# Joining the key-value sums of batches 2 and 3 with neighbouring matmul groups, and loading their q and k into the narrowing's memory

## The chip, the cores and the metric

The kernel runs on one core of one Trainium2 chip. The metric is the time of one execution on the device in microseconds (us), the median of several runs. The engines are named as in the profile: PE is TensorE, DVE is VectorE, ACT is ScalarE, POOL is GpSimd, and SP is SyncE, which here issues DMAs only.

## What is computed

The reference has two parts, one after the other. The first is an attention with polynomial sketches over 4 batches and 4 heads, with 1088 positions of 32 values:

```python
def phi(x):
    a = np.einsum('rd,bhsd->bhsr', S1, x)      # r = 8
    b = np.einsum('rd,bhsd->bhsr', S2, x)
    return np.einsum('bhsi,bhsj->bhsij', a, b).reshape(*x.shape[:-1], r * r)
q_p, k_p = (phi(q), phi(k))
kv = np.einsum('bhsf,bhsd->bhfd', k_p, v)
z = np.sum(k_p, axis=2)
num = np.einsum('bhsf,bhfd->bhsd', q_p, kv)
den = np.einsum('bhsf,bhf->bhs', q_p, z)[..., None] + 1e-06
attn = num / den
```

The second takes the result as 4352 tokens of 128 values (`x`) through a gated layer with 1536 inner columns:

```python
gate = 1.0 / (1.0 + np.exp(-(x @ w_gate)))
val = x @ w_val
out = gate * val @ w_out
```

All of it is in 32-bit floats. The inputs arrive as 64-bit numbers, so the weights are narrowed on the chip first.

## The kernel before

**The gated layer sets the rhythm.** The tokens are cut into chunks of 512 (the last has 256). For each chunk, the 1536 inner columns are taken in blocks of 128. One block of one chunk is a wave: `w1` multiplies `xT` with the blocks of `w_gate` and `w_val` into a PSUM tile `wave` (line 540), ACT takes the sigmoid (line 548), and DVE multiplies the two into `g` (`glu`, line 583). There are 12 waves in a chunk and 102 in all. Counting starts at 0, so chunk 2 is waves 24 to 35. The PSUM pool `psm` has two buffers for `wave` tiles, and two small groups of attention matmuls (`cqps` and `nps`) take a turn in it as well.

**The second product follows later.** For chunks 1 to 7, `w2_a` and `w2_b` multiply `g` with `w_out` in seven half-sized products in place of eight (`prod`, line 377). They need sums of token halves, which POOL makes (`tsum`, line 367). They run three and four waves after the second wave of a pair. When a chunk is complete, DVE puts the pieces together in several small sums and two transposes (lines 479 and 514, tiles `res` and `o_sb`). These stand in the list `moe["late"]`, and one entry is taken per wave.

**The order is written by hand.** The program fixes the order of PE, DVE, ACT and POOL. The order in which SP issues its DMAs is chosen by a planner. `slot(group, waves)` first emits a group of attention work, then for each wave the `glu` of the wave before, one entry of `late`, the second products that are due, and the next wave. `until(n)` emits waves until n have been emitted, so a step after `until(n)` stands on DVE between `glu(n-2)` and `glu(n-1)`. Here "slot n" is the place just ahead of wave n. A chunk's waves may start only when its tokens are in `xT`.

**Attention of one batch** passes through these steps:

- `load_kq` and `load_v` fetch k, q and v. The tile for k and q (tag `kq`, one buffer) is also the tile `bq` of the q features.
- `turn_k` and `turn_q` transpose k and q on DVE (lines 642 and 653).
- `begin`: `kps` projects k in 16 matmul records (line 673), and DVE transposes the result into `kab`. `qcomp` projects q (`cqps`, line 819), ACT copies the result to `cq`, and `spread` writes it to DRAM (`dq`) and reads it back repeated, in 14 DMAs on SP, into `qp`, `bq`, `a8` and `b8`.
- `outer` makes the k features on DVE (line 752, twice). `sum_z` adds them up over positions (line 926, one instruction and then three).
- `kv` multiplies the features with v (lines 892 and 901) into a tile of the PSUM pool `ps2` (tag `two`, one buffer of two banks). `kvd` copies that out on ACT (line 914).
- `ndt` transposes the copy (lines 957 and 965). `weights_z` prepares the denominators' weights on DVE (lines 1001 to 1008).
- `qmult` completes the q features on DVE (line 872, twice).
- `parts` makes the denominators (`den_j`, line 1021, with a DVE product at line 1029, then line 1034), the numerators (line 1258), and the quotients in `xT`.

**The plan of batches 2 and 3** is a table of wave numbers, one for each of `turn_k`, `turn_q` twice, `begin`, `outer` twice, `sum_z` twice, `kv`, `qmult` with `ndt` and `weights_z`, `qmult`, and `parts`:

```python
plan = {2: (27, 29, 30, 31, 32, 34, 36, 37, 38, 39, 42, 44)}
plan[3] = (48, 49, 51, 53, 56, 57, 58, 59, 60, 61, 63, 68)
```

**The narrowing** of the weights works in the tiles `cap`, `tail` and `head` of the pool `sbN`, until a step in the waves of chunk 0 completes the last block. The pool stays reserved to the end.

**At the start** `warm` issues matmuls with constants, whose result nobody reads.

Of the kernel before, what the change touches and what calls it, by code (L numbers as in the profile page):

```python
# [16 lines left out]
P = 128  # L17
# [3 lines left out]
def kernel(  # L21
# [31 lines left out]
    ld = ctx.enter_context(tc.tile_pool(name="ld", bufs=1))  # L53
    sbA = ctx.enter_context(tc.tile_pool(name="sbA", bufs=2))
    raw = ctx.enter_context(tc.tile_pool(name="raw", bufs=NJ // 2))
    sbN = ctx.enter_context(tc.tile_pool(name="sbN", bufs=1))
    sbG = ctx.enter_context(tc.tile_pool(name="sbG", bufs=3))

    dram = ctx.enter_context(tc.tile_pool(name="dram", bufs=1, space=bass.MemoryType.DRAM))

# [203 lines left out]
    k_t, q_t = {}, {}  # L264


    def new_kq(b):
        t = ld.tile([P, 2 * H * W1], F32, tag="kq", name="kq")
        kq = t[:, : 2 * T * D].rearrange("p (a t d) -> p a t d", a=2, t=T)
        k_t[b], q_t[b] = kq[:, 0], kq[:, 1]  # L270

# [20 lines left out]
    def warm(*cols):  # L292
        t = psm.tile([P, 2, 512], F32, tag="wave", name="warm")
        x = nc.const_aps.tensor(1.0, [P, P], F32)
        for n in cols:
            r = nc.const_aps.tensor(1.0, [P, n], F32)
            nc.tensor.matmul(out=t[:, 0, :n], lhsT=x, rhs=r, start=True, stop=True)  # L297
# [312 lines left out]
    def slot(group, waves, behind=None):  # L610

        if group is not None:
            group()
        todo = moe["todo"]
        for _ in range(waves):
            more = moe["ci"] < len(tok_chk)
            if more and sum(tok_chk[moe["ci"]]) > moe["ready"]:
                break
            glu()
            for _ in range(2 if moe["ci"] >= len(tok_chk) - 1 else 1):  # L620
                if moe["late"]:
                    moe["late"].pop(0)()
            while todo and todo[0][0] <= moe["n"]:
                todo.pop(0)[1]()
            if behind is not None:
                behind()
                behind = None
            if more:
                w1()
            elif not todo:  # L630
                break
            else:
                todo.pop(0)[1]()
# [26 lines left out]
    WD = 160  # L660
    mask = {}

    def kps(b):
        t = ps2.tile([P, 2, 512], F32, tag="two", name="kps")
        ts = [t[:, 0], t[:, 1]]
        turns = [(g, pi) for g in range(4) for pi in range(2)]

        if b == 0:
            ts[1] = pso.tile([P, TCH], F32, tag="acc1", name="kps1")
            turns.sort(key=lambda x: x[1])  # L670
        for g, pi in turns:
            rows = slice(64 * pi, 64 * pi + 64)
            nc.tensor.matmul(  # L673
                out=ts[pi][32 * g : 32 * g + 32, : NJK * 32],
                lhsT=sk[rows, :],
                rhs=kT_of[b][rows, KBASE[g] : KBASE[g] + NJK],
                start=True,
                stop=True,
            )

        KAB[b] = sbA.tile([P, 2, NJK, 32], F32, tag="kab", name="kab")
        for pi in range(2):
            nc.vector.transpose(
                out=KAB[b][:, pi].rearrange("p j c -> p (j c)"), in_=ts[pi][:, : NJK * 32]
            )
        KP[b] = sbA.tile([P, 2, NJK, 2, F], F32, tag="kp", name="kp", bufs=1)
# [147 lines left out]
    def spread(b, ns, cq, put, get):  # L834
        p0 = 64 * ns[0]
        d = dram.tile([P, 2, W1], F32, tag="dq", name="dq")
        put.dma_start(out=d[p0:], in_=cq[p0:])
        for n in ns:
            for i, t in enumerate((QP[b], BQ[b])):

                for c in (0, 1) if i else (0,):
                    d0 = d[64 * n + 32 * c + 2 * i, 0]
                    rows = [[0, R], [8 * W1, R]] if i else [[8 * W1, 2 * R], [0, R]]
                    get.dma_start(  # L844
                        out=t[64 * c : 64 * c + 64 if i else P, n * H * W1 : (n + 1) * H * W1],
                        in_=bass.AP(
                            tensor=d0.tensor, offset=d0.offset, ap=rows + [[1, H * W1]]
                        ),
                    )
        if len(ns) < 2:  # L850
            return
        put = get

        B8[b] = sbA.tile([P, W1], F32, tag="b8", name="b8", bufs=1)
        A8[b] = sbA.tile([P, 2, WD], F32, tag="a8", name="a8", bufs=1)
        for x in range(2):
            for m in range(2):
                p0 = 64 * x + 32 * m
                for i, t in enumerate((A8[b], B8[b])):
                    d0 = d[2 * i + m, 0]  # L860
                    if i == 0:
                        offset, run = d0.offset + (W1 - WD) * x, [[W1, 2], [1, WD]]
                    else:
                        offset, run = d0.offset + W1 * x, [[1, W1]]
                    put.dma_start(
                        out=t[p0 : p0 + 32],
                        in_=bass.AP(tensor=d0.tensor, offset=offset, ap=[[8 * W1, 32]] + run),
                    )
# [16 lines left out]
                    skip_group_check=True,  # L885
                )

    def kv(b, zsum):
        kvz = KVZ[b] = ps2.tile([P, 2, 512], F32, tag="two", name="kvz")[:, 0]
        for j in [1, 2, 3, 4, 5, 6, 7, 8, 0]:  # L890
            for h in range(H):
                nc.tensor.matmul(  # L892
                    out=kvz[32 * h : 32 * h + 32, :F],
                    lhsT=v_sb[:, h, j, :],
                    rhs=KP[b][:, h // 2, j, h % 2, :],
                    start=(j == 1),
                    stop=(j == 0),
                    skip_group_check=True,
                )
        for h in range(H):  # L900
            nc.tensor.matmul(
                out=kvz[32 * h : 32 * h + 32, F : 2 * F],
                lhsT=nc.const_aps.tensor(1.0, [P, 32], F32),
                rhs=zsum[:, h, :],
                start=False,
                stop=True,
                skip_group_check=True,
            )
# [104 lines left out]
        )  # L1013


    def den_j(b):
        t = ps2.tile([P, 2, 512], F32, tag="two", name="denj")
        for pi in range(2):
            rows = slice(64 * pi, 64 * pi + 64)
            for x in range(4):  # L1020
                nc.tensor.matmul(  # L1021
                    out=t[32 * x : 32 * x + 32, pi, :WD],
                    lhsT=ZW[b][rows, 4 * (x % 2) : 4 * (x % 2) + 4].rearrange("p x i -> p (x i)"),
                    rhs=B8[b][rows, (W1 - WD) * (x // 2) : (W1 - WD) * (x // 2) + WD],
                    start=True,
                    stop=True,
                )
        PD[b] = sbA.tile([P, 2, WD], F32, tag="pd", name="pd", bufs=1)
        nc.vector.tensor_tensor(out=PD[b], in0=t[:, :, :WD], in1=A8[b], op=MUL)


    def den_i(b, dps):
# [118 lines left out]
        start=True,  # L1151
        stop=True,
    )
    warm(64)
    st_ = st_[:, : 2 * R].rearrange("p (n r) -> p n r", n=2)
    sk = const.tile([P, 2, 2, R], F32, tag="sk")
    nc.vector.tensor_tensor(
# [71 lines left out]
    slot(None, 1)  # L1229
    cq = {}  # L1230

    def begin(b):
        glu()
        kps(b)
        cq[b] = qcomp(b, (0, 1), (psm, "wave"))
        spread(b, (0, 1), cq[b], nc.scalar, nc.sync)

# [6 lines left out]
    def part01(first):  # L1244
        glu()
        late.append(dn(0, 1)(first=first, later=True))
# [16 lines left out]
                    stop=True,  # L1263
                )

    def parts(b):
        den_j(b)
        glu()
        t = psm.tile([P, 2, 512], F32, tag="wave", name="nps")
        numerators(b, t, False)  # L1270
# [38 lines left out]
    load_kq(1)  # L1309
    slot(None, 1)  # L1310
    slot(lambda: part01(lambda: narrow_w(NJ - 1, 3)), 1)
    slot(last01, 1)
    load_v(1)
    turn_k(1)
    slot(None, 1)
    turn_q(1, 0)
# [14 lines left out]
    slot(lambda: ndt(1), 1)  # L1331
    slot(None, 1)
    qmult(1, 1)
    load_kq(2)
    slot(None, 1)
    slot(lambda: parts(1), 1)
    moe["store"]()
# [1 line left out]
    def until(n):  # L1339
        slot(None, n - moe["n"])  # L1340

    plan = {2: (27, 29, 30, 31, 32, 34, 36, 37, 38, 39, 42, 44)}
    plan[3] = (48, 49, 51, 53, 56, 57, 58, 59, 60, 61, 63, 68)
    for b in range(2, B):
        at = iter(plan[b])
        until(next(at))
        turn_k(b)
        for n in range(2):
            until(next(at))
            turn_q(b, n)  # L1350
        until(next(at))
        slot(lambda: begin(b), 1)
        for pi in range(2):
            until(next(at))
            outer(b, pi)
        for step in range(2):
            until(next(at))
            sum_z(b, step)
        until(next(at))
        slot(lambda: kv_all(b), 1)  # L1360
        if b + 1 < B:
            load_v(b + 1)
        until(next(at))
        qmult(b, 0)
        slot(lambda: ndt(b), 1)
        weights_z(b)
        until(next(at))
        qmult(b, 1)
        load_kq(b + 1)
        until(next(at))  # L1370
        slot(lambda: parts(b), 1)
    slot(None, 10**3)


# [28 lines left out]
```

## Time and profile before

| | |
|---|---|
| median of 3 runs | 292.19 us (292.1 to 292.46) |
| profiled execution, its own time | 296.02 us |
| span of the profiled execution, first to last instruction | 294.1 us |
| PE busy | 288.8 us, 98% of the span |
| DVE busy | 186.5 us, 63% |
| POOL busy | 160.6 us, 55% |
| ACT busy | 93.7 us, 32% |
| DMA | 24.23 MB, mean 82 GB/s |
| granted clock of PE, mean | 0.999 |

The busy times come from one profiled execution. Its own time is longer than the median of the runs, so its durations are read against its own span. Matmuls overlap, and the ends of their rows are modelled. For PE, therefore, the distances between starts say more than the sums of durations. A row of the order in time has the start from the span's beginning, the duration, the engine, the line, the operation, what it writes and reads, and in brackets how long the engine was idle before it and what ended that.

### The profile page before, as it was taken

The numbers are of one execution on the slowest core, as the hardware profiler recorded it, in microseconds if no ns is written. First come the engines' busy times: TensorE is split into PE (matmuls) and PEld (weight loads), VectorE is DVE, ScalarE is ACT, GpSimd is POOL, SyncE is SP. The second block draws the span as 40 slices with busy tenths as digits, with TensorE's granted clock in tenths as the row PEclk, the third lists the DMA queues.
The fourth block names the chain that finished last, engine by engine and source line by source line (L and its number), as shares of the span: only waits on it lengthen the run. The fifth ranks groups of instructions, "written<-read, shape, count | busy, mean of one in ns | idle before, by whom it ended". The sixth has DMA issues, their size and how long they took to land.

```text
span 294.1 us, 5762 instructions
## 1 busy us (share of the span) xinstructions
PE 288.8 (98%) x2264; PEld 156.6 (53%) x2264; DVE 186.5 (63%) x316; ACT 93.7 (32%) x172; POOL 160.6 (55%) x222
## 2 busy tenths in 40 slices
PE   8989999999999999999999999999999999999995
PEld 3543433355455455545555555554555555555895
DVE  5778789885656766677556696667436423552482
ACT  3386542321324222323224222323223223322321
POOL 2266544796535657655456498555456565646300
PEclk9999999999999999999999999999999999999999
DMA  7993613295640168416000474202000200020003
GB/s 219 347 336 68 150 39 125 74 180 137 186 97 0 19 163 159 133 50 177 12 0 2 129 174 106 37 0 38 1 0 2 36 2 0 0 31 7 0 4 54
DMA packets 28890, 24.23 MB, mean 82 GB/s; under 512 B 18560, under 2 KB 24064, under 8 KB 28864
## 3 DMA queue, kind: packets, MB, share of 16 engines
q1 hardware_dynamic: 25808, 21.95, 30.1%
q10 hardware_dynamic: 3056, 1.92, 2.3%
q8 instruction: 18, 0.29, 0.4%
q14 instruction: 8, 0.07, 0.1%
HBM read 20.60 MB, written 3.26 MB: 81 GB/s over the span
## 4 chain that ended last, share of the span: by engine, by line
PE 89%; DMA 7%; SPq 1%; DVE 0%; issue 0%; ACT 0%; DVEq 0%
PE wave L540 55%; PE prod L377 20%; DMA bq<-dq 5%; PE moeout L421 4%; PE moeout L447 2%; PE warm L297 1%; PE kps L673 1%; SPq L844 1%; PE nps L1258 1%; DMA s_in<-in_S_dram 1%; PE kvz L892 1%; PE cqps L819 1%; DMA dq<-cq 1%; DMA b<-dq 1%; PE denj L1021 0%; PE dps L1063 0%
## 5 line engine op out<-in xcount | busy, mean ns | idle before, releaser
L540 PE MATMUL wave<-xT,w_sb 128*64 128x512 f32 (+3 forms) x820 | 210.6, 566 | 0.0
L540 PEld LDWEIGHTS wave<-xT,w_sb 128*64 128x64 f32 (+1 forms) x820 | 85.4, 140 | 63.2 <-issue 51.0
L548 ACT ACTIVATE sg<-wave 128x512 f32<-128x512 f32 x102 | 60.9, 597 | 171.1 <-PE wave L540 163.2
L583 DVE TENSOR_TENSOR g<-wave,sg 128x512 f32<-128x512 f32 x96 | 65.9, 686 | 76.3 <-ACT sg L548 75.0
L367 POOL TENSOR_TENSOR tsum<-g 128x256 f32<-128x256 f32 x84 | 67.9, 810 | 29.7 <-DVE g L583 29.6
L367 POOL TENSOR_TENSOR tsum<-g,tsum 128x256 f32<-128x256 f32 x42 | 34.2, 814 | 57.8 <-DVE g L583 57.6
L377 PE MATMUL prod<-tsum,ws 128*64 128x256 f32 x252 | 62.8, 381 | 0.0
L377 PEld LDWEIGHTS prod<-tsum,ws 128*64 128x64 f32 x252 | 31.2, 137 | 16.0 <-issue 11.8
L377 PE MATMUL prod<-g,w_sb 128*64 128x256 f32 x168 | 34.7, 381 | 0.0
L367 POOL TENSOR_TENSOR tsum<-tsum,g 128x256 f32<-128x256 f32 x42 | 32.7, 779 | 3.3
L377 PE MATMUL prod<-tsum,w_sb 128*64 128x256 f32 x84 | 25.3, 383 | 0.0
L377 PEld LDWEIGHTS prod<-g,w_sb 128*64 128x64 f32 x168 | 16.0, 136 | 17.5 <-issue 14.7
L377 PE MATMUL prod<-g,ws 128*64 128x256 f32 x84 | 25.0, 379 | 0.0
L117 POOL TENSOR_TENSOR head<-head,tail 128x384 int32<-128x384 int32 (+1 forms) x10 | 9.9, 987 | 13.9 <-DVE head L111 12.6
L377 PEld LDWEIGHTS prod<-g,ws 128*64 128x64 f32 x84 | 11.5, 137 | 3.7
L421 PE MATMUL moeout<-g,w_sb 128*128 128x512 f32 (+1 forms) x28 | 12.5, 603 | 0.0
L377 PEld LDWEIGHTS prod<-tsum,w_sb 128*64 128x64 f32 x84 | 10.8, 137 | 3.0 <-issue 2.2
L872 DVE TENSOR_TENSOR qp<-qp,bq 128x1152 f32<-128x1152 f32 (+1 forms) x7 | 9.4, 1344 | 4.6 <-DMA a<-dq 4.6
L752 DVE TENSOR_TENSOR kp<-kab 128x1152 f32<-128x1152 f32 (+2 forms) x10 | 10.9, 1101 | 0.0
L576 DVE TENSOR_TENSOR g<-wave,sg 128x512 f32<-128x512 f32 x6 | 6.7, 1121 | 4.6 <-ACT sg L548 4.6
L479 DVE TENSOR_TENSOR res<-prod,other 64x512 f32<-64x512 f32 (+1 forms) x14 | 7.6, 544 | 3.1 <-DMA a<-dq 1.6
L514 DVE STREAM_TRANSPOSE o_sb<-res 64x512 f32<-64x512 f32 x14 | 9.6, 688 | 0.0
(129 smaller groups left out, 209.6 us busy)
## 6 DMA issues: line engine op xcount, KB each, us to landing
qp<-dq SPq DMA_DIRECT2D x7, 576.0 KB
bq<-dq SPq DMA_DIRECT2D x14, 288.0 KB
kq<-in_k_dram SPq DMA_DIRECT2D x3, 544.0 KB
kq<-in_q_dram SPq DMA_DIRECT2D x3, 544.0 KB
w_in<-in_moe_w_out_dram SPq DMA_DIRECT2D x6, 256.0 KB
w_in<-in_moe_w_gate_dram SPq DMA_DIRECT2D x5, 256.0 KB
w_in<-in_moe_w_val_dram SPq DMA_DIRECT2D x5, 256.0 KB
v<-in_v_dram SPq DMA_DIRECT2D x8, 144.0 KB
```

The source lines that it names most:

```text
L117: nc.gpsimd.tensor_tensor(out=head, in0=head, in1=tail, op=ALU.add)
L367: nc.gpsimd.tensor_tensor(out=t[:, u], in0=in0, in1=in1, op=ALU.subtract)
L377: nc.tensor.matmul(out=out, lhsT=lhsT, rhs=rhs, start=start, stop=stop, skip_group_check=True)
L421: nc.tensor.matmul(out=moe["acc"][d], lhsT=w_sb[:, 2, j, d], rhs=g[:, jj], start=(j == 0), stop=(j == NJ - 1),)
L479: nc.vector.tensor_tensor(out=out, in0=in0, in1=in1, op=op)
L514: nc.vector.transpose(out=o_sb[:64, d].rearrange("p t x -> p (t x)"), in_=r[:, 1 + 2 * d : 3 + 2 * d].rearrange("p u x -> p (u x)"),)
L540: nc.tensor.matmul(out=wv[d, which, jj * tw + o : jj * tw + o + tp], lhsT=w_sb[:, which, j0 + jj, d], rhs=xT[:, t0 + o : t0 + o + tp], sta ...
L548: nc.scalar.activation(out=sg, in_=wv[:, 0], func=ACTF.Sigmoid)
L576: nc.vector.tensor_tensor(out=g.rearrange("p (j u s y) -> p j y u s", j=2, u=2, y=4), in0=wv[:, 1].rearrange("p (j y u s) -> p j y u s", j ...
L583: nc.vector.tensor_tensor(out=g, in0=wv[:, 1], in1=sg, op=MUL)
L752: eng.tensor_tensor(out=KP[b][:, pi, j0:j1].rearrange("p j m (i l) -> p (j m) i l", i=R), in0=bass.AP(tensor=a0.tensor, offset=a0.offset, ...
L872: nc.vector.tensor_tensor(out=q0, in0=q0, in1=half(BQ[b], n), op=MUL)
```

## The change

- `kv` of batch 2 is issued inside `begin` of batch 3, right before `kps`, into free columns of the same `two` tile. Its copy `kvd` follows `kps`.
- `kv` of batch 3 is issued inside `parts` of batch 2, right before `den_j`, into free columns of that `two` tile. There `glu` of the wave before now comes ahead of `den_j`, and `kvd` follows the DVE product.
- k and q of batches 2 and 3 get a tile of their own, `kq2`, in a pool `late` that takes the memory of `sbN` once the narrowing is done. `a8` and `b8` of batch 3 are there too. k and q of batch 2 are loaded ahead of batch 1's transposes, and those of batch 3 after batch 2's.
- The table of wave numbers becomes a written-out order. Batch 3's steps move forward, in between those of batch 2.
- One `warm` matmul at the start has 128 columns in place of 64.

| step | batch 2 before | batch 2 after | batch 3 before | batch 3 after |
|---|---|---|---|---|
| `turn_k`, `turn_q` twice | 27, 29, 30 | 25, 26, 27 | 48, 49, 51 | 34, 35, 36 |
| `begin` | 31 | 28 | 53 | 37 |
| `outer` twice | 32, 34 | 29, 31 | 56, 57 | 39, 40 |
| `sum_z` twice | 36, 37 | 32, 33 | 58, 59 | 41, 42 |
| `kv` | 38 | 37 | 60 | 45 |
| `weights_z`, `ndt` | 39 | 38 | 61 | 48 |
| `qmult` twice | 39, 42 | 40, 43 | 61, 63 | 50, 52 |
| `parts` | 44 | 45 | 68 | 56 |

```diff
+    late_pool = []
     def new_kq(b):
-        t = ld.tile([P, 2 * H * W1], F32, tag="kq", name="kq")
+        pool, tag, w = (ld, "kq", 2 * H * W1) if b < 2 else (late_pool[0], "kq2", 2 * T * D)
+        t = pool.tile([P, w], F32, tag=tag, name="kq")
...
-    def kps(b):
+    def kps(b, also=None):
         t = ps2.tile([P, 2, 512], F32, tag="two", name="kps")
+        if also is not None:
+            kv(also, ZS[also], t[:, 0, NJK * 32 : NJK * 32 + 2 * F])
...
-        B8[b] = sbA.tile([P, W1], F32, tag="b8", name="b8", bufs=1)
-        A8[b] = sbA.tile([P, 2, WD], F32, tag="a8", name="a8", bufs=1)
+        pool = late_pool[0] if b == B - 1 else sbA
+        B8[b] = pool.tile([P, W1], F32, tag="b8", name="b8", bufs=1)
+        A8[b] = pool.tile([P, 2, WD], F32, tag="a8", name="a8", bufs=1)
...
-    def kv(b, zsum):
-        kvz = KVZ[b] = ps2.tile([P, 2, 512], F32, tag="two", name="kvz")[:, 0]
+    def kv(b, zsum, kvz=None):
+        if kvz is None:
+            kvz = ps2.tile([P, 2, 512], F32, tag="two", name="kvz")[:, 0]
+        KVZ[b] = kvz
...
-    def den_j(b):
+    def den_j(b, also=None):
         t = ps2.tile([P, 2, 512], F32, tag="two", name="denj")
+        if also is not None:
+            kv(also, ZS[also], t[:, 0, 2 * WD : 2 * WD + 2 * F])
...
         nc.vector.tensor_tensor(out=PD[b], in0=t[:, :, :WD], in1=A8[b], op=MUL)
+        if also is not None:
+            kvd(also)
...
-    warm(64)
+    warm(128)
...
-    def begin(b):
+    def begin(b, also=None):
         glu()
-        kps(b)
+        kps(b, also)
+        if also is not None:
+            kvd(also)
...
-    def parts(b):
-        den_j(b)
+    def parts(b, also=None):
+        if also is not None:
+            glu()
+        den_j(b, also)
         glu()
...
     slot(lambda: part01(lambda: narrow_w(NJ - 1, 3)), 1)
+    top.close()
+    late_pool.append(ctx.enter_context(tc.tile_pool(name="late", bufs=1)))
     slot(last01, 1)
     load_v(1)
+    load_kq(2)
     turn_k(1)
...
     qmult(1, 1)
-    load_kq(2)
...
+    turn(2, 25, 26, 27)
+    load_kq(3)
+    until(28)
+    slot(lambda: begin(2), 1)
+    features(2, 29, 31, 32, 33)
+    turn(3, 34, 35, 36)
+    until(37)
+    slot(lambda: begin(3, 2), 1)
+    load_v(3)
+    until(38)
+    weights_z(2)
+    slot(lambda: ndt(2), 1)
+    until(39)
+    outer(3, 0)
+    until(40)
+    outer(3, 1)
+    qmult(2, 0)
+    until(41)
+    sum_z(3, 0)
+    until(42)
+    sum_z(3, 1)
+    until(43)
+    qmult(2, 1)
+    until(45)
+    slot(lambda: parts(2, 3), 1)
+    until(48)
+    weights_z(3)
+    slot(lambda: ndt(3), 1)
+    until(50)
+    qmult(3, 0)
+    until(52)
+    qmult(3, 1)
+    until(56)
+    slot(lambda: parts(3), 1)
```

`turn` and `features` call the transposing steps, and `outer` and `sum_z`, at the given waves. The loop that the table drove is removed.

More of the change, by code (lines that the diff above doesn't have):

```diff
@@ L55 @@
     raw = ctx.enter_context(tc.tile_pool(name="raw", bufs=NJ // 2))
-    sbN = ctx.enter_context(tc.tile_pool(name="sbN", bufs=1))
     sbG = ctx.enter_context(tc.tile_pool(name="sbG", bufs=3))
+    top = ExitStack()
+    sbN = top.enter_context(tc.tile_pool(name="sbN", bufs=1))
     dram = ctx.enter_context(tc.tile_pool(name="dram", bufs=1, space=bass.MemoryType.DRAM))
@@ L1340, in until, with turn, features @@
         slot(None, n - moe["n"])
[L1342 to L1371, printed above, removed]
+    def turn(b, *at):
+        for n, step in zip(at, (turn_k, lambda b: turn_q(b, 0), lambda b: turn_q(b, 1))):
+            until(n)
+            step(b)
+    def features(b, *at):
+        steps = [(outer, 0), (outer, 1), (sum_z, 0), (sum_z, 1)]
+        for n, (step, i) in zip(at, steps):
+            until(n)
+            step(b, i)
+    turn(2, 25, 26, 27)
[32 more added lines that the diff above has]
+    slot(lambda: parts(3), 1)
     slot(None, 10**3)
```

## The prediction

> **What bounds the kernel now.** I read the page first (busy times, then the chain that ended last), then the waits of TensorE, then the order of TensorE's and VectorE's instructions in time.
>
> ```profile
> PE 288.8 (98%) x2264; PEld 156.6 (53%) x2264; DVE 186.5 (63%) x316; ACT 93.7 (32%) x172; POOL 160.6 (55%) x222
> PE 89%; DMA 7%; SPq 1%; DVE 0%; issue 0%; ACT 0%; DVEq 0%
> ```
> ```profile
> PE denj L1021 <- DMA b<-dq: 0.4, 1, 0.4
> ```
> TensorE is the bound from about 20 us to the end: every 10 us stretch there but 70 to 80 has it fully busy. Its listed waits sum to 2.0 us; only `denj` of batch 1, at 75.9, lies in the steady part. So a step gains only if it takes time out of TensorE's own stream, and loses as soon as it makes a wave wait.
>
> The pace comes from the plain stretch late in the kernel: wave 72 starts at 213.42 and wave 84 at 243.17, so 29.75 / 12 = **2.48 us a wave** (1.72 us of `wave` matmuls and half of two waves' `prod` matmuls).
>
> A wave writes one of two PSUM buffers of `psm`. Wave n+2 can start when VectorE has ended `glu` of wave n (L583). Over these waves `glu` ends 3.3 to 3.7 us after its wave starts, and the next user of the buffer starts 1.4 to 1.5 us later. A start has come as close as 0.18 us after the end. So VectorE may be about **1.2 us late** before TensorE waits.
>
> VectorE's average of 63% hides where it is dense. These are its instructions behind waves 39 to 42, in order (start, duration):
>
> ```profile
> 128.05 0.67 DVE L479 TENSOR_TENSOR res<-prod,res 64x512 f32<-64x512 f32 x1
> 128.64 0.41 DVE L479 TENSOR_TENSOR res<-prod,other 64x256 f32<-64x256 f32 x1
> 130.11 0.69 DVE L583 TENSOR_TENSOR g<-wave,sg 128x512 f32<-128x512 f32 x1 [1.05 <-ACT sg L548]
> 130.71 0.41 DVE L479 TENSOR_TENSOR res<-res,other 64x256 f32<-64x256 f32 x1
> 131.15 1.10 DVE L479 TENSOR_TENSOR res<-res 64x512 f32<-64x512 f32 x1
> 132.18 1.34 DVE L872 TENSOR_TENSOR qp<-qp,bq 128x1152 f32<-128x1152 f32 x1
> 133.45 0.67 DVE L583 TENSOR_TENSOR g<-wave,sg 128x512 f32<-128x512 f32 x1
> ```
> The `res` rows are the sums that close token chunk 2. They come once per 12 waves, here in slots 38 to 43, whatever attention does. One `qmult` (132.18) beside them already makes the next `glu` 0.8 us late; TensorE is not touched.
>
> **What the Trainium skill says.** "TensorEngine Tiling (Array Packing)", Key Properties: changing the tiling mode drains TensorE. The trace agrees: the eight `wave` matmuls take 1.72 us before another 64-column group and 1.87 us before `kps`, `kvz` or `denj`, 0.15 more. "SBUF — State Buffer", Who interferes with whom: a VectorE instruction with two SBUF inputs and a GpSimd one that reads SBUF take turns on a shared port. The trace shows a spread that fits: the L752 product at 1.31 to 1.71 us, the first L926 sum at 1.22 to 1.50. "TensorE: Matmul & The Clock Gate", What's actually happening: half clock until an activity window of some 3.4 us was busy; here the record of full clock begins 13.6 us into the span.
>
> **The change, part by part.**
>
> Joined groups. `kv` of a batch is 72 + 8 matmul records:
>
> ```profile
> 179.42 1.21 PE L892 MATMUL kvz<-kp,v 128*32 128x64 f32 x72
> 180.45 0.29 PE L901 MATMUL kvz<-zs,const-float32-1.0 128*32 128x64 f32 x8
> 180.67 0.65 PE L377 MATMUL prod<-g,w_sb 128*64 128x256 f32 x4
> ```
> 180.67 - 179.42 = 1.25 us on TensorE, and that stays. What goes is one way in and out of 32-column mode per join. From wave 48 to 60 the kernel takes 181.59 - 149.14 = 32.45 us; less 29.75 of plain pace, less `kps` and `cqps` (1.13) and `kvz` (1.25), leaves 0.32 for two ways in and out, 0.16 each. The step from `kv` (128 rows) to `kps` or `denj` (64 rows) is itself a change of mode that no row shows; it gives back between none and all of it. Upper bound of the gain, counting 0.15 in and 0.11 out for each: 0.5. I take **-0.2 us** for both joins, bounds -0.5 and +0.2.
>
> `glu` before `den_j(2)`: 0.69 on VectorE while TensorE does the new `kv(3)`; the product with `a8` was to follow `denj` anyway, and `denj` is later than `glu` by the 1.25 of `kv`. Nothing. `kvd` on ScalarE (0.37) lies in 68% idle; `ndt(2)`, which reads it and needs the `two` bank free, comes a full wave later. Nothing, up to 0.2.
>
> `warm(128)`: the `warm` pair of 64 columns stands at 5.68 to 6.37, and `kps` of batch 0 starts at 6.30, 0.2 after its input `sk` (5.97 + 0.14). The 512-column pair at 11.29 takes about 1.9, so 64 columns more in both passes cost up to 0.23; some of it hides in the wait for `sk`. **+0.1**, bounds 0 and +0.25; a gain through the clock is a rival below.
>
> Loads. k and q of a batch were issued at 42.14 and landed by 47.71: 5.2 us for 1.09 MB. k and q of batch 2 wait for the narrowing's last VectorE product (45.63 + 0.93 = 46.6), then land by about 53, in front of batch 1's `dq` write at 54.6; covered, 1.6 us to spare. If SP takes them later they push that batch's `b` tiles, for which `denj` waits today. k and q of batch 3 move from 133.6 to about 92.5, where SP has no DMA from 78.1 to 101.1; `spread(2)` (14 DMAs, 17.4 us from 105.55 to 122.9) moves to some 98 to 116 with it, and its first reader, `qmult(2,0)` in slot 40, is 10 us later. `bq` has one buffer, so `spread(3)` stops on SP until `qmult(2,1)` of slot 43, then needs some 17 us, to about 155; its halves for `qmult(3,0)` of slot 50 land by about 146. v of batch 3 is behind it in the program, but SP follows readiness, not the text: v of batch 1 went at 17.87, ahead of `spread(0)` at 28.69, which stands earlier in the code. Nothing. POOL's queue holds only token sums, paced by `glu`; their products come three waves later.
>
> VectorE's order. Batch 2's steps stay near their waves, but all of batch 3's features move from waves 48 to 59 into waves 34 to 42, among batch 2's `qmult` steps and the sums that close chunk 2. Instructions are the same; what changes is who waits behind whom. The longest run is from `glu(38)` to `glu(41)`, with these durations, start to start where rows touch:
>
> ```profile
> 169.38 1.31 DVE L752 TENSOR_TENSOR kp<-kab 128x1152 f32<-128x1152 f32 x1
> ...
> 123.55 1.24 DVE L872 TENSOR_TENSOR qp<-qp,bq 128x1024 f32<-128x1024 f32 x1
> ...
> 114.04 1.22 DVE L926 TENSOR_TENSOR z<-kp 128x1024 f32<-128x1024 f32 x1
> ...
> 116.48 0.68 DVE L926 TENSOR_TENSOR z<-z 128x512 f32<-128x512 f32 x1
> 117.19 0.83 DVE L926 TENSOR_TENSOR zs<-z 128x256 f32<-128x256 f32 x1
> 118.06 0.83 DVE L926 TENSOR_TENSOR zs<-zs,kp 64x256 f32<-64x256 f32 x1
> ```
> A chunk sum 0.36; `outer(3,1)` 1.25; `qmult(2,0)` 1.17; `glu(39)` 0.61; two chunk sums 0.97; `sum_z(3,0)` 1.15; `glu(40)` 0.61; two chunk sums 1.47; `sum_z(3,1)` 2.34 (116.48 to 118.82); `glu(41)` 0.69. Together 10.6 us. `glu(38)` ends about 3.6 us after wave 38 starts (3.3 in its own row; `ndt` now stands in that slot). So `glu(41)` ends at 14.2. Wave 43, which takes its buffer, is due at 5 x 2.48 = 12.4 and needs the end 0.2 earlier: it waits 14.2 - 12.2 = **+2.0 us**. With the dearest rows for L752 and L926 (1.71, 1.50, and 2.56 in batch 3) the run is 11.6 and the wait 3.0; with `glu(38)` at 3.3 and a sharp hand-over it is 1.5. TensorE has nothing else to do in it: its queue is in order. What is late next is `glu(42)`, behind a transpose (0.63) and `qmult(2,1)` (1.27); after the wait it just meets wave 44. In waves 25 to 36 the same counting gives at most 0.6 us of lateness, below 1.2. Batch 3's later steps (slots 48 to 56) meet chunk 3's sums with only two `qmult`, as batch 2 does now.
>
> **Sum:** -0.2 + 0.1 + 2.0 = +1.9 us. On the profiled execution's own time, 296.02 (span 294.1 and 1.9 around it), that is 297.9; it was 3.8 above the median of the runs, and I carry the difference over: 292.19 + 1.9 = **294.1**. What a measurement can tell from no change is 0.2%, 0.6 us.
>
> **Rivals.**
> *The run is hidden.* If wave 43's slack or the rows are kinder by 1.8 us, only the small terms stay: 292.0 to 292.3, no change. For it: in slots 38 to 44 of the kernel before no wave waited. Against: 10.6 us of work in order, all with rows, against three waves' 7.4 and 1.2 of slack. 0.11.
>
> *An earlier full clock*, the one that ends faster. If the added `warm` columns make one more activity window count as busy, the clock rises 3.4 us sooner, at about 10.2. TensorE's rows from 10.2 to 13.6 (`bps`, `gram`, the 512-column `warm`) run at half rate; half of them is up to 1.6 us. It decides once the wait at wave 43 is below 1.1 us. For it: `kps` of batch 0 takes 1.14 us, later 0.51. Against: 64 columns are little in a window already nine tenths busy. Then 291.3. 0.09.
>
> *A transfer comes late.* SP takes v of batch 3 behind the stopped `bq`, or k and q of batch 2 into batch 1's spread. The second costs up to 5.2 us at `denj(1)`, the first some 10 us at `kv(3)` in slot 45. Against: the order seen at 17.87. With the wait: 297 to 304. 0.08.
>
> **Numbers.** Forecast 0.72, its own range 293.0 to 295.3. Faster 0.09, same 0.11, slower 0.80. For eight in ten the range goes from 292.0, which takes in the hidden case, to 296.0.
>
> **What would show it.** In the changed profile: a TensorE gap before wave 42 or 43, `glu(41)` starting 5 us or more after its wave instead of 2.9, VectorE without idle from slot 39 to 43; `kvz` straight before `kps` and `denj` with less than 0.15 in between; `bq` of batch 3 waiting on L872. No gap there and a median below 292.8 would make the prediction wrong; so would a wait for v, or for `b` longer than today's.

## The result, and the profile after

| | before | after |
|---|---|---|
| median of the runs compared | 292.38 us (292.10 to 292.75, 6 runs) | 294.94 us (294.64 to 298.69, 6 runs) |
| ratio | | 1.0109, interval 1.006 to 1.0158 |
| profiled execution, its own time (span) | 296.02 (294.1) | 294.88 (293.1) |
| start of wave 24 | 84.07 | 80.62 |
| start of wave 72 | 213.42 | 212.36 |
| **stage from wave 24 to wave 72** | **129.34** | **131.74** |

The kernel became 1.1% slower, 2.6 us between the medians, with 294.1 predicted. The two spans say the opposite. The profiled execution of before got TensorE's full clock 13.6 us into the span, while in every other profile of this study the clock was full after 3.7 to 7.0 us. Wave 12 starts at 49.95 us in it and at 47.2 to 48.3 in the others, so the spans of these two profiles cannot be compared. All that the change moves, apart from `warm` and the first loads, lies between waves 24 and 72, and both of those waves start in clean stretches. The stage between them is the measure used below. It repeats to 0.01 us between profiles of kernels that do not differ in it (129.34 in before, e1 and e8; 131.74 and 131.73 in after and e2). Ahead of it, the start of wave 12 varies by about 1 us, and the way from wave 12 to wave 24 by another 0.8 (33.1 to 33.9 us, the profile of before left out). So the stage lost **2.40 us**, and it is this that has to be explained.

The page of after, its busy times and the shares of the chain by engine:

```profile
PE 285.4 (97%) x2264; PEld 156.5 (53%) x2264; DVE 188.2 (64%) x316; ACT 93.8 (32%) x172; POOL 169.4 (58%) x222
PE 79%; DVE 9%; DMA 7%; POOL 2%; issue 1%; SPq 1%; ACT 1%; POOLq 0%; DVEq 0%
```

VectorE's share of the chain went from 0% to 9% with the same 316 instructions. Its busy share of the whole moved by one point, and nothing in that number warns of the change. TensorE's waits of after (engine and line, what it waited for, then us in total, times, longest) show where VectorE entered the chain:

```profile
PE prod L381 <- DVE res L483: 0.9, 1, 0.9
PE wave L544 <- DVE g L587: 0.8, 1, 0.8
PE nps L1273 <- ACT kvd L923: 0.2, 1, 0.2
```

None of the three is there before. The one listed before, `denj` for `b`, is gone from after's list; it lay ahead of wave 24 and varies between profiles (0.3 in e4, not listed in e5). The first two lie in one stretch of 10 us, the third 7.6 us behind the second. VectorE's order in time in that stretch, from `glu(39)` to the second `qmult` of batch 2 (start, duration, engine, line, operation):

```profile
126.01 0.68 DVE L587 TENSOR_TENSOR g<-wave,sg 128x512 f32<-128x512 f32 x1
126.61 0.67 DVE L483 TENSOR_TENSOR res<-prod,res 64x512 f32<-64x512 f32 x1
127.21 0.41 DVE L483 TENSOR_TENSOR res<-prod,other 64x256 f32<-64x256 f32 x1
127.54 1.21 DVE L935 TENSOR_TENSOR z<-kp 128x1024 f32<-128x1024 f32 x1
...
130.74 1.21 DVE L935 TENSOR_TENSOR z<-z 128x512 f32<-128x512 f32 x1
131.99 0.84 DVE L935 TENSOR_TENSOR zs<-z 128x256 f32<-128x256 f32 x1
132.87 0.83 DVE L935 TENSOR_TENSOR zs<-zs,kp 64x256 f32<-64x256 f32 x1
133.63 0.67 DVE L587 TENSOR_TENSOR g<-wave,sg 128x512 f32<-128x512 f32 x1
134.23 0.69 DVE L518 STREAM_TRANSPOSE o_sb<-res 64x512 f32<-64x512 f32 x1
134.85 1.79 DVE L879 TENSOR_TENSOR qp<-qp,bq 128x1152 f32<-128x1152 f32 x1
```

No row has a bracket, so VectorE has no idle time in it: this is the predicted run. TensorE's order of after holds the two answers:

```profile
127.76 0.40 PE L381 MATMUL prod<-tsum,ws 128*64 128x256 f32 x1 [0.94 <-DVE res L483]
...
134.36 1.94 PE L544 MATMUL wave<-xT,w_sb 128*64 128x512 f32 x8 [0.76 <-DVE g L587]
```

- **Slot 41.** The next `prod` starts 2.82 us after the last seven matmuls of wave 40 begin (127.76 - 124.94). It is the first product of chunk 3 into the PSUM accumulator `acc1`, which the pool `pso` has once. It waits until the sums of chunk 2 that read `acc1` have ended, the two `res` rows up to 127.62. In plain pace it follows after 1.73 (127.47 to 129.20 at the same place in before), so the wait is 1.09.
- **Wave 43.** `glu(41)` ends at 134.30 and wave 43 starts at 134.36. Its last products took 1.79 us to the start of the wave, 0.81 in plain pace: 0.98.
- **Wave 44.** The same distance is 1.17 against 0.86, because `glu(42)` stands behind the `qmult` of 1.79: 0.31.

Together 2.38 us. The group that contains `den_j` also holds a new wait of 0.40. Its last numerators (`nps`, 64 x 32) stand still until the copy `kvd` is done, so that the next step, `den_i`, starts 1.49 us after the first numerators (142.21 - 140.72); without the join it is 1.09:

```profile
140.72 1.06 PE L1273 MATMUL nps<-qp,nd 64*32 64x512 f32 x16
141.98 0.30 PE L1273 MATMUL nps<-qp,nd 64*32 64x32 f32 x16 [0.20 <-ACT kvd L923]
142.21 0.49 PE L1047 MATMUL nps<-pd,head 128*64 128x160 f32 x4
```

The joins give some of this back. These small terms needed experiments.

### The profile page after: what moved, and what is told of

Its sections match the earlier page's. It is cut to its first block, busy times and chain, and to the rows that moved or that the text cites. A ratio compares the mean times of both kernels' runs of the same rounds, so it can differ in the third digit from the quotient of the medians.

```text
span 293.1 us, 5758 instructions
## 1 busy us (share of the span) xinstructions
PE 285.4 (97%) x2264; PEld 156.5 (53%) x2264; DVE 188.2 (64%) x316; ACT 93.8 (32%) x172; POOL 169.4 (58%) x222
## 4 chain that ended last, share of the span: by engine, by line
PE 79%; DVE 9%; DMA 7%; POOL 2%; issue 1%; SPq 1%; ACT 1%; POOLq 0%; DVEq 0%
PE wave L544 51%; PE prod L381 20%; DMA w_in<-in_moe_w_gate_dram 2%; POOL head L118 2%; PE moeout L451 2%; DMA v<-in_v_dram 2%; DMA w_in<-in_moe_w_out_dram 1%; DVE qp L879 1%; PE moeout L425 1%; DVE res L483 1%; DVE w_sb L127 1%; DVE head L112 1%; DMA kq<-in_k_dram 1%; DVE z L935 1%; DVE kp L758 1%
## 5 line engine op out<-in xcount | busy, mean ns | idle before, releaser
L371 POOL TENSOR_TENSOR tsum<-g 128x256 f32<-128x256 f32 x84 | 73.2, 875 | 22.1 <-DVE g L587 22.0
L381 PE MATMUL prod<-tsum,ws 128*64 128x256 f32 x252 | 61.8, 381 | 0.9 <-DVE res L483 0.9
L371 POOL TENSOR_TENSOR tsum<-tsum,g 128x256 f32<-128x256 f32 x42 | 36.1, 860 | 3.3
L381 PE MATMUL prod<-g,w_sb 128*64 128x256 f32 x168 | 33.9, 381 | 0.0
L381 PEld LDWEIGHTS prod<-g,ws 128*64 128x64 f32 x84 | 11.5, 137 | 3.6
```

The costliest lines, as they stand in the source:

```text
L371: nc.gpsimd.tensor_tensor(out=t[:, u], in0=in0, in1=in1, op=ALU.subtract)
L381: nc.tensor.matmul(out=out, lhsT=lhsT, rhs=rhs, start=start, stop=stop, skip_group_check=True)
```

## The experiments

Two theories stood against each other. The first: VectorE's run among the sums of chunk 2 makes TensorE wait, and the places of the steps decide. The rivals: the joins, the extra copy, the loads or the longer `warm` cost time of their own. In the expectations, "stage" is the time from wave 24 to wave 72. Every ratio is against the kernel before, on the same chip.

### e1, e2: the longer `warm` alone, and the change without it

```diff
-    warm(64)      # e1: before with
+    warm(128)
-    warm(128)     # e2: after with
+    warm(64)
```

> The kernel before with the one warm matmul of 128 columns. If VectorE's run in slots 39 to 43 is the loss, this costs what the prediction gave it: 0 to +0.25 us against the kernel before. If the longer warm were part of the loss, +0.5 or more. If it brings the full clock a window earlier, 1.6 us or more less than the kernel before in every run, and the record of full clock begins near 10 us instead of 13.6.

> The changed kernel with the warm matmul back at 64 columns. VectorE's run as the loss: still 2.3 to 2.7 us slower than the kernel before, within 0.25 us of the changed kernel. The start as the loss: it comes back to within 1 us of the kernel before.

e1: 292.86 us, ratio 0.9989 (0.9968 to 1.0009), stage 129.34, full clock from 5.06 us. e2: 295.59 us, ratio 1.0088 (1.0072 to 1.0104), stage 131.73, full clock from 4.96 us. Neither the loss nor the early clock depends on the `warm` columns. e1's profile also gives the span of the kernel before with an early clock, 290.6 us; after's 293.1 is 2.5 above it, which agrees with the medians.

### e3, e4: one VectorE step moved out of the run

```diff
     until(38)
     weights_z(2)
+    qmult(2, 0)          # e3
...
     until(40)
     outer(3, 1)
-    qmult(2, 0)          # e3
     until(41)
     sum_z(3, 0)
-    until(42)            # e4
-    sum_z(3, 1)          # e4
     until(43)
     qmult(2, 1)
+    until(44)            # e4
+    sum_z(3, 1)          # e4
```

> The changed kernel with qmult(2,0), 1.2 us on VectorE, moved from slot 40 to slot 38, where VectorE was idle; nothing else. VectorE's run as the loss: the run is 1.2 us shorter, so the wait of prod in slot 41 goes from 1.5 to 0.3 us and the sum of waits up to wave 43 from 2.2 to 1.0; the time is 1.0 to 1.3 us below the changed kernel's. Joins or loads as the loss: no change.

> The changed kernel with sum_z(3,1), 2.9 us on VectorE, moved from slot 42 to slot 44; nothing else. It tells the two hand-overs apart. The prod of slot 41 waits for chunk 2's sums, which stand ahead of sum_z(3,1), so its 1.5 us stay; the waits for glu(41) and glu(42), 1.0 and 0.3 us, go. 1.0 to 1.3 us below the changed kernel. If only the wave buffers mattered, the whole 2.2 us would go; if joins or loads were the loss, nothing would.

e3: 293.61 us, ratio 1.0028 (1.0017 to 1.0040), stage 130.16, which is 1.58 less than after. e4: 294.18 us, ratio 1.0040 (1.0024 to 1.0056), stage 130.40, 1.34 less. TensorE's order of e3, then of e4:

```profile
133.16 1.08 PE L544 MATMUL wave<-xT,w_sb 128*64 128x512 f32 x4 [0.34 <-DVE g L587]
```
```profile
128.61 0.40 PE L381 MATMUL prod<-tsum,ws 128*64 128x256 f32 x1 [0.93 <-DVE res L483]
```

With `qmult(2,0)` out from in front of the sums of chunk 2, the wait for `acc1` is gone, and wave 43 waits 0.34 where it waited 0.76. With `sum_z(3,1)` out, both waves are on time and the wait for `acc1` stays as it was; it is what e4 has left of the loss (130.40 - 129.34 = 1.06). So the two waits have two causes in one run, and each step pays for its own. The expectations had put the wait at slot 41 at 1.5 us; against plain pace it is 1.09. e3 gave more than was expected of it; two steps behind the moved one got shorter as well: the last add of `sum_z(3,1)` took 0.42 us in place of 0.83, and `qmult(2,1)` 1.31 in place of 1.79.

### e5: all of batch 3's steps spread out

```diff
     until(37)
+    qmult(2, 0)
...
     until(38)
     weights_z(2)
+    outer(3, 0)
...
     until(39)
-    outer(3, 0)
+    qmult(2, 1)
     until(40)
     outer(3, 1)
-    qmult(2, 0)
     until(41)
     sum_z(3, 0)
-    until(42)
+    until(44)
     sum_z(3, 1)
-    until(43)
-    qmult(2, 1)
```

> The changed kernel with VectorE's steps spread out: qmult(2,0) in slot 37, outer(3,0) in 38, qmult(2,1) in 39, outer(3,1) in 40, sum_z(3,0) in 41, sum_z(3,1) in 44. Joins, loads and the warm matmul stay. VectorE's run as the loss: no wait in slots 40 to 44, 2.5 to 2.9 us below the changed kernel, within 0.4 us of the kernel before. Joins as the loss: still 1 us or more slower than the kernel before.

292.51 us, ratio 0.9998 (0.9989 to 1.0008), stage 129.31: 2.43 less than after, and level with before. Nothing but places on VectorE was changed. Wave by wave, the distances in after and e5 agree to 0.01 us except in the three places named above: 1.09 from wave 40 to 41, 0.98 from 42 to 43 and 0.36 from 43 to 44, which make up the 2.43. Busy time by stretch, of after and then of e5 (stretch, length, PE, PEld, DVE, ACT, POOL, clock, DMA share, GB/s):

```profile
125.00:135.00 10.00, 8.30 (x49) 4.12 (x47) 9.90 (x14) 1.79 (x3) 8.82 (x7) 1.00 0.41 85
```
```profile
125.00:135.00 10.00, 10.00 (x63) 5.65 (x61) 8.22 (x12) 2.39 (x4) 9.12 (x10) 1.00 0.71 165
```

In after VectorE is busy for 99% of this stretch and TensorE for 83%; in e5 it is 82% and 100%. GpSimd is as busy in e5 (9.12 us) as in after (8.82), so its load alone is not what TensorE waited for. The loss is the order of VectorE's steps; all else that the change does cancels to 0.03 us.

### e6: `kvd` ahead of the VectorE product

The copy `kvd` of batch 3 and the product `pd` on VectorE read the same `two` tile. In after, `kvd` starts late, and TensorE's last numerators wait for it. ScalarE's order of after:

```profile
141.56 0.37 ACT L923 COPY kvd<-denj 128x256 f32<-128x256 f32 x1 [1.67 <-DVE pd L1040]
```

Its input was complete at about 140.4, where the next group starts. The copy itself starts when VectorE's `pd` has ended (141.52). e6 is e5 with the two exchanged:

```diff
-        PD[b] = ...
-        nc.vector.tensor_tensor(out=PD[b], in0=t[:, :, :WD], in1=A8[b], op=MUL)
         if also is not None:
             kvd(also)
+        PD[b] = ...
+        nc.vector.tensor_tensor(out=PD[b], in0=t[:, :, :WD], in1=A8[b], op=MUL)
```

> The respaced kernel with the ScalarE copy of kv of batch 3 (kvd) ahead of the VectorE product PD in den_j. In the changed kernel kvd waits for PD and the last 16 numerator records wait for kvd: nps takes 1.49 us there, 1.09 in the kernel before. If that order is the cause, nps is back at 1.1 and the time 0.3 to 0.5 us below the respaced kernel. If the copy's place doesn't matter, equal to it.

292.51 us, ratio 0.9997 (0.9986 to 1.0008), stage 129.31: no gain. The expectation was not met. From the first `nps` to the `den_i` product it still takes 1.49 us, and the wait only has another name:

```profile
PE nps L1272 <- DVE pd L1042: 0.2, 1, 0.2
```

The two readers go one after the other in either order (in e6 `kvd` runs from 139.49 to 139.86 and `pd` starts at 139.89), and the numerators' second tile waits for the later one. What keeps the two apart, no run shows.

### e7: e5 without the joins; e8: the loads alone

```diff
     turn(3, 34, 35, 36)
+    slot(lambda: kv_all(2), 1)          # e7, kv of batch 2 by itself
     until(37)
     qmult(2, 0)
-    slot(lambda: begin(3, 2), 1)
+    slot(lambda: begin(3), 1)
...
     until(45)
-    slot(lambda: parts(2, 3), 1)
+    slot(lambda: kv_all(3), 1)
+    until(46)
+    slot(lambda: parts(2), 1)
```

e8 is the kernel before with the pool `late`, k and q of batches 2 and 3 in it, and their loads issued at the places in the order where after issues them. `a8` and `b8` of batch 3 stay where they were, unlike what its expectation says; they are in `late` in after and in all the runs built on it.

> The respaced kernel with both joins undone: kv of batch 2 as its own group in slot 36, kv of batch 3 in slot 45, parts of batch 2 in slot 46. If a join saves the way in and out of the 32-column mode, this is 0.2 to 0.5 us slower than the respaced kernel, less the 0.4 us that nps waits for kvd there. If joins cost, it is faster by more than 0.4.

> The kernel before with its own order of steps and only the loads changed: q and k of batches 2 and 3 and a8, b8 of batch 3 in the narrowing's memory, q and k of batch 2 loaded ahead of batch 1's transposes, those of batch 3 after batch 2's. Hidden loads: equal to the kernel before within 0.3 us. Loads as part of the loss: +0.5 to +5 us, with denj of batch 1 waiting longer for its b tiles than 0.9 us.

e7: 292.75 us, ratio 0.9992 (0.9971 to 1.0013), stage 129.50. The joins are therefore worth 0.19 us net (129.50 - 129.31), the other slots that `kv` and `parts` have in e7 included. In e7 the numerators take 1.09 us and in e5 1.49, so the joins gain 0.59 by this difference and lose 0.40 of it again to `kvd`. e7 is 0.16 above before in the stage; its cause stays open. e8: 292.45 us, ratio 0.9997 (0.9989 to 1.0006), stage 129.34. The loads cost nothing.

### e9, e10, e11: a better place for `kv(3)`

After e6 the remedy is a tile of the group in which the copy has no second reader ahead of TensorE. `den_i` is the second step of the denominators, and `ndps` in the expectations is the tile that `ndt` writes. e9 issues `kv(3)` behind the last numerators, into the second bank of their tile, still ahead of `den_i`. e10 is e9 with `weights_z` and `ndt` of batch 2 one slot later. e11 is e9 with `den_i` ahead of `kv(3)` and without the early `glu`.

```diff
     def parts(b, also=None):
-        if also is not None:
-            glu()
-        den_j(b, also)
+        den_j(b)
...
         numerators(b, t[:, :, WD : WD + 32], True)
-        turn_den(b, den_i(b, t[:, 0, :WD]))
+        den_i(b, t[:, 0, :WD])
+        if also is not None:
+            kv(also, ZS[also], t[:, 1, 256 : 256 + 2 * F])
+        turn_den(b, t[:, 0, :WD])
+        if also is not None:
+            kvd(also)
```

(e11 against e5. e9 keeps the early `glu` and has `den_i` between `kvd` and `turn_den`. In all three the copy `num` of batch 2 lies in the pool `late`, since `kp` is still being read.)

> The respaced kernel with kv of batch 3 moved, within parts(2, 3), from ahead of den_j to behind the last numerators, into bank 1 of their tile; the numerators' copy gets memory of the pool late, since kv now reads the features after it. If two readers of one PSUM bank taking turns (PD on VectorE, kvd on ScalarE) cost the 0.4 us in nps, nps is back at 1.1 us, and waves 24 to 72 take 128.9 us instead of 129.31. If the 0.4 us come from going from 128-row to 64-row matmuls, nps stays at 1.5 and the stage at 129.3. The whole time within 0.5 us of the kernel before either way.

> The kernel with kv of batch 3 last, and also weights_z and ndt of batch 2 in slot 39 instead of 38. In the changed kernel, slot 38 spends 0.26 us more around ndps than slot 39 of the kernel before. If that hangs on where the two column halves of the array stand when ndps begins, slot 39 gives it back: waves 24 to 72 in 128.6 us. If it is ndps itself, the stage stays at 128.9. VectorE's run gets longer by 0.7 us of weights_z and should still end in time: no wait for glu.

> The respaced kernel with kv of batch 3 as the last matmuls of parts(2, 3), behind the denominators (den_i), without the glu ahead of den_j that kv covered, and with the numerators' copy in the pool late. In the kernel with kv behind the numerators, nps waited for PD (0.6 us, glu ahead of it on VectorE was no longer covered) and den_i for kvd (0.5). If those two are the whole of its loss of 1.0 us, both go: nps takes 1.1 us instead of the 1.49 of the respaced kernel, and one more change of mode (0.15) comes in, so waves 24 to 72 take 129.0 to 129.1 us, 0.3 less than the kernel before (129.34) and the respaced one (129.31). If kv so late makes VectorE's quotients late, wave 45 or 47 waits and the stage is at 129.5 or more.

e9: 293.91 us, ratio 1.0039 (1.0020 to 1.0058), stage 130.33, 1.02 more than e5. The expectation was not met. Two waits of TensorE, both new:

```profile
PE nps L1268 <- DVE pd L1038: 0.6, 1, 0.6
PE nps L1042 <- ACT kvd L923: 0.5, 1, 0.5
```

The early `glu` now stands in front of `pd` with no `kv` on TensorE to cover it, and `den_i`, which goes into the same tile, waits for the copy of `kv`. e10: 294.98 us, ratio 1.0074 (1.0057 to 1.0092), stage 131.50, 1.17 more than e9; its expectation was not met either. The 0.7 us of `weights_z` now stand just ahead of `qmult(2,1)`, which takes 1.90 us there. Behind it stands the last sum of chunk 2 that reads the other accumulator, `acc0`, and the first product of chunk 3 into `acc0` waits for that sum in slot 40. The two rows, VectorE's and TensorE's:

```profile
124.86 0.40 DVE L483 TENSOR_TENSOR res<-prod,res 64x256 f32<-64x256 f32 x1
```
```profile
125.41 0.65 PE L381 MATMUL prod<-g,w_sb 128*64 128x256 f32 x4 [1.01 <-DVE res L483]
```

The slot of `ndps` itself changes nothing: from wave 37 to wave 39 e9 takes 5.37 us and e10 too. So it is not this slot that makes e7 0.16 slower than before.

e11: 292.40 us, ratio 0.9989 (0.9980 to 0.9999), stage 129.05, as expected. TensorE's order of e11:

```profile
136.89 0.50 PE L1030 MATMUL denj<-b,zw 64*32 64x160 f32 x16
137.19 1.16 PE L1268 MATMUL nps<-qp,nd 64*32 64x512 f32 x32
138.27 0.49 PE L1042 MATMUL nps<-pd,head 128*64 128x160 f32 x4
138.69 1.21 PE L901 MATMUL nps<-kp,v 128*32 128x64 f32 x72
```

The numerators run in one piece of 1.08 us, `den_i` in 0.42, and `kv` follows without a gap. This version is 0.3 us below before in the stage of its one profile and 0.4 us in the median (292.40 against 292.79). The interval of the ratio just excludes no change, and the size is below the 0.2% that a measurement can tell well, so the stage is the better evidence of the two. Against the change as made, its stage is 2.69 us shorter.

## Why the prediction was right, and which terms were off

**The run on VectorE: right in kind, 2.0 predicted, 2.38 measured.** It placed the end of `glu(41)` 14.2 us after the start of wave 38; it came after 14.5 (134.30 - 119.78). The wave started here:

```profile
119.78 1.61 PE L544 MATMUL wave<-xT,w_sb 128*64 128x512 f32 x6
```

The order in time shows the steps that it added up, without idle. Up to wave 43 the waits make 2.07 us, against 2.0 predicted; the other 0.31 came at wave 44. Three details were wrong:

- The prediction saw one resource, the `wave` buffers, and put the whole wait at wave 43. Of the 2.38 us, 1.09 were waited earlier, in slot 41, for the accumulator `acc1`. The sums of chunk 2 free it, and the prediction counted those sums as load without asking who waits for them. The total barely changes, for a wait taken at slot 41 shortens the one at wave 43 by as much. It agrees although one of the two waits was not foreseen. The cure does change: e4 alone cannot remove the wait at slot 41.
- "After the wait it just meets wave 44" failed by 0.31: `qmult(2,1)` took 1.79 us where 1.27 was used.
- `sum_z(3,1)` took 2.89 us from its start to `glu(41)` (133.63 - 130.74), where the rows of batch 2 gave 2.34. The first of its three adds took 1.21 in place of 0.68. This is more than the 2.56 that the prediction held ready for its upper bound; the other steps of the run are within 0.04 us of what it had given them. Its sum for that bound, 11.6, is 11.5 from its own rows.

**The joins: -0.2 predicted, -0.19 measured, and by luck, since two errors cancel.** The gain before the loss to `kvd` is 0.59 us, above the stated bound of 0.5. The step from 128 to 64 rows gave nothing back: `kps` behind `kv` takes 0.51 us to `cqps`, as it does when it stands alone.

```profile
113.85 1.21 PE L901 MATMUL kps<-kp,v 128*32 128x64 f32 x72
114.88 0.29 PE L910 MATMUL kps<-zs,const-float32-1.0 128*32 128x64 f32 x8
115.10 0.72 PE L679 MATMUL kps<-kT,sk 64*32 64x288 f32 x16
115.61 0.69 PE L825 MATMUL cqps<-qT,skq 64*32 64x288 f32 x16
```

**`kvd`: "nothing, up to 0.2" predicted, 0.40 measured.** The cover that was named, ScalarE's idle 68% and `ndt(2)` a wave later, belongs to the copy of batch 2, and there it held. For the copy of batch 3 the prediction did not ask who takes the tile next. That copy was not late for want of ScalarE; it had to wait for another reader of its tile, and the next user of the tile was not `ndt` but the numerators of the same group.

**`warm`: +0.1 predicted, none measured** (e1, -0.11% with -0.32 to +0.09). **Loads: nothing predicted, none measured** (e8). The 5.2 us that it gives for k and q count from the second issue, at 42.55; from the first, at 42.14, they are 5.6. SP's order was as predicted. In after, v of batch 3 is issued ahead of the stopped `bq`:

```profile
115.04 1.88 SPq L256 DMA_DIRECT2D v<-in_v_dram  x4
...
136.67 2.47 SPq L850 DMA_DIRECT2D bq<-dq  x4
```

136.67 follows the end of `qmult(2,1)` (134.85 + 1.79 = 136.64), so the `bq` buffer was the stop, and `kv` of batch 3 did not wait for v.

**The sum.** -0.2 + 0.1 + 2.0 stood for +1.9; the stage shows +2.40, the medians +2.6. The wait was 0.4 too small. The rest cancels to -0.03: -0.19 for the joins, and the +0.16 of e7 whose cause is open.

**The rivals.** *The run is hidden* fell: the waits are there, and e5 shows what it takes to hide them. *An earlier full clock* fell as a mechanism: the clock is early with 64 columns too (4.96 us in e2), and e1 was not faster. *A transfer comes late* fell by the rows above.

## What to carry to other kernels

An engine at 64% of the whole can be the bound for 10 us: take its steps in order between two deadlines, add up their durations, and compare with the time until the buffer is due. Do this for every buffer that the steps in the run set free, the accumulators too, and not only for the one with the shortest cycle. When two pieces of work are put into one PSUM tile, list all readers of that tile and what on TensorE comes next for it: of the 0.59 us saved on the switch of mode, 0.40 were lost to a copy that came second.

## What the runs showed of the hardware that was not expected

- The same VectorE instruction varies with its surroundings: the last add of `sum_z(3,1)` took 0.83 us in after and 0.42 in e5, and `qmult(2,1)` 1.34 in e5, 1.79 in after and 1.90 in e10. The page "SBUF — State Buffer" of the Trainium skill, which the prediction drew on (Who interferes with whom), would fit the adds. In the 13 profiles, the two adds that write `zs` took 0.42 to 0.43 us in all 13 cases in which GpSimd did nothing beside them, and 0.83 to 0.84 in all 65 in which it did. The products do not follow so simply: in before, the one of line 752 took 1.31 us both with GpSimd idle (at 104.18) and with GpSimd busy all through it (at 169.38). So the spread that the prediction quotes for that line is no sign of it. No run was made to test the cause.
- The stage between two waves repeats to 0.01 us between profiles, while the start of wave 12 alone varies by about 1 us. A few tenths can be read from one profile if the stage is cut at clean starts.
- The start of the full clock lay at 13.6 us in one profile and at 3.7 to 7.0 in the others, two of which have the same `warm` (4.96 in e2, 6.97 in e8). Wave 12 started 1.7 to 2.8 us later in that one. TensorE had been busy for 12.7 of the 12.8 us from its first matmul to the full clock there, so the busy window of some 3.4 us that the prediction uses does not account for it. A profiled execution that is 3.6 us above the median of its runs (296.02 against 292.38) asks for a look at the start before its span is compared.
